# One fp32 product for the attention scores in place of three products of split halves, in a fused attention and gated-MLP kernel

## Chip, cores and metric

The kernel runs on one core of one Trainium2 chip. The metric is the device time of one execution in microseconds (us), the median of three runs. The engines are named as the profile names them: PE is TensorE's matmul side and PEld its weight loads, DVE is VectorE, ACT is ScalarE, POOL is GpSimd, SP is SyncE, which only issues DMAs here. Everything is fp32 in memory. A tile typed fp32r holds fp32 words whose products the kernel takes at TensorE's reduced precision; a product of plain fp32 tiles is taken at full precision.

## The reference

```python
B, H, S, D = (4, 8, 576, 64)
scores = scale * np.matmul(q, k.transpose(0, 1, 3, 2))        # scale = 1/8
scores = np.where(causal, -1000000000.0, scores)
scores = scores - scores.max(-1, keepdims=True)
a = np.exp(scores); a /= a.sum(-1, keepdims=True) + 1e-09
local = np.matmul(a, v)
phi = lambda x: np.where(x > 0, x, np.exp(x) - 1.0) + 1.0
mem_out = (phi(q) @ M_prev) / (phi(q) @ z_prev + 1e-6)
out = g * mem_out + (1 - g) * local                           # g = sigmoid(beta), one per head
x = out as [2304 tokens, 512]
y = (silu(x @ w_gate) * (x @ w_val)) @ w_out                  # d_ff = 1536
```

The attention has 32 heads of 576 positions and 64 features; the MLP has 2304 tokens.

## The kernel before

The attention loop takes two heads at a time: 16 pairs, numbered 0 to 15, and one more turn (16) that only finishes the last. Partitions 0 to 63 of a pair's tiles hold the features of its first head and 64 to 127 those of its second. `pair_load` brings raw queries `qr` (128x768: the last 64 positions twice, positions 0 to 511, then the last 64 of both heads laid out block-diagonally) and raw keys `kr` (128x576). Each is held in `NR` = 2 buffers.

`pair_split` makes of each raw tile a high half (`qh`, `kh`, the value rounded to fp32r) and a low half (`ql`, `kl`, the rest). High and low together carry nearly full fp32 precision, so a score is the sum of three one-pass products, high x high, high x low and low x high: `self.products` lists them, and each accumulates in one PSUM bank. For pair 0 the work is cut in two and lies on ACT, POOL and DVE; for every other pair all four operations lie on POOL, but for pair 1's `kh`, which is ACT's.

Scores come in five tiles of 128 query rows. `scores(t)` for t = 0 to 3 takes the keys up to the diagonal, 128(t+1) columns, both heads side by side: head 0 uses rows 0 to 63 of TensorE and head 1 rows 64 to 127, each with a bank of its own (64*128 in the trace). `scores4` does the last 64 rows of both heads at once with all 128 rows, twice 288 keys (128*128). DVE reads each bank with the mask and takes the row's extreme (`reading`), ACT takes the exponential with the row sum (`exp`), POOL multiplies by the reciprocal sum and the gate (`scaled`).

A turn of the loop is software-pipelined: while pair n's scores are made, pair n-1's weights are transposed by TensorE against `ident` (`turned1`, `turned`), evacuated to `g`, and multiplied with the values (`values`, tiles `g,vp`), its memory part comes from `recall` (`mm,ph`: phi(q) times the memory matrix, in plain fp32), and its result leaves as `xh` and `xl`. `phi_parts` computes the feature map phi(q) of pair n+1 from raw `qr`: two activations on ACT (`qe`, `ph`) and one DVE operation. PE, ACT, DVE and POOL each run their instructions in the order in which the Python code issues them: the wrapper `queued` links each instruction to the one before on its engine (its recording line is L92 in the profile, so rows are told apart by tile names). SP's DMAs are ordered by the tile scheduler.

So TensorE's order within a turn is: scores t = 0 and 1, transposes of the old pair's `ps` and `pl`, `mm,ph`, scores t = 2 and 3, more transposes, `scores4`, transposes of `p` and `mem`, and the products `g,vp`. The loads of pair n+2 are issued at the end of turn n. After the loop come the MLP's products, also of split halves, which the change does not touch.

Of the kernel before, what the change touches and what calls it, by code (L numbers as in the profile page):

```python
# [9 lines left out]
F32 = mybir.dt.float32  # L10
F32R = mybir.dt.float32r
# [3 lines left out]
ALU = mybir.AluOpType  # L15
# [14 lines left out]
ORDER = (0, 768, 1536)  # L30
EARLY, AHEAD = (2, 6, 10, 14), (1, 5, 9, 11, 12, 13, 14)
PLAIN = 3
ACT_K = (0, 1)
ON_POOL = ("q", "k")
PS_S, PS_T = 4, 4
NBIG, NSMALL, FB, NK, NR, NM, NX = 8, 8, 2, 2, 2, 2, 2
STEPS = ("p1", "p2", "p6", "p7", "p5", "p4", "p3")
EDGE_A, EDGE_B, EDGE_X = 16, 176, 40
TCKW = dict(schedule_with_timeline_sim=True)
# [7 lines left out]
def attention_moe(ctx: ExitStack, tc: tile.TileContext, qt, kt_, v, m, beta, wg, wv, wo, out):  # L47
# [22 lines left out]
    def follow(ins, other, why, kind=mybir.DependencyClass.NoSync):  # L70
        tc.add_manual_dep(
            getattr(ins, "ins", ins), getattr(other, "ins", other).name,
            mybir.DependencyInfo(kind, mybir.DependencyReason.DATA), reason=why,
        )
# [26 lines left out]
    pe, act, dve, pool = queued(PE), queued(ACT), queued(DVE), queued(POOL)  # L101

    def rot(pool, name, shape, dtype, n, off=0):
        held = slots.setdefault(name, [0, []])
        if len(held[1]) < n:
            free, at = math.prod(shape[1:]), f"{name}{len(held[1])}"
            if off or free % 64:
                whole = pool.tile([shape[0], -(-(off + free) // 64) * 64], dtype, name=at)[:, off : off + free]
                held[1].append(whole if len(shape) == 2 else whole.rearrange("p (a b) -> p a b", b=shape[2]))
            else:  # L110
                held[1].append(pool.tile(shape, dtype, name=at))
        held[0] += 1
        return held[1][(held[0] - 1) % n]

    def kept(pool, name, shape, dtype, n):
        for _ in range(n):
            rot(pool, name, shape, dtype, n)

    def split_hi(dst, src):
        return pool.tensor_scalar(dst, src, 1.0, 0.0, op0=ALU.mult, op1=ALU.add)  # L120

    def split_lo(dst, src, hi, kind=""):
        eng = pool if kind in ON_POOL else dve
        return eng.tensor_tensor(dst, src, hi.bitcast(F32), op=ALU.subtract)

    ident = const.tile([128, 128], F32, name="ident")
    make_identity(nc, ident)
# [13 lines left out]
    for hh in range(2):  # L141
        rows = slice(hh * 64, hh * 64 + 64)
# [133 lines left out]
    with tc.tile_pool(name="sb", bufs=1, reuse_waits="tile") as sb:  # L276
# [21 lines left out]
            SP.dma_start(vp, v[b, pr])  # L298
            return vp

        def pair_split(n, raw):
            qr, kr = raw
            q = [rot(sb, f"q{part}", [128, 640], F32R, NK) for part in "hl"]
            k = [rot(sb, f"k{part}", [128, 576], F32R, NK, 16) for part in "hl"]
            if n == 0:
                cuts = [(slice(0, 256), slice(0, 256)), (slice(256, 576), slice(256, 640))]
                lo = lambda dst, src, hi: dve.tensor_tensor(dst, src, hi.bitcast(F32), op=ALU.subtract)
                raw = qr[:, 128:768]
                for ck, cq in cuts:
                    act.copy(k[0][:, ck], kr[:, ck])  # L310
                    split_hi(q[0][:, cq], raw[:, cq])
                (ck, cq), (dk, dq) = cuts
                lo(k[1][:, ck], kr[:, ck], k[0][:, ck])
                lo(q[1][:, cq], raw[:, cq], q[0][:, cq])
                lo(k[1][:, dk], kr[:, dk], k[0][:, dk])
                return q, k, lambda: lo(q[1][:, dq], raw[:, dq], q[0][:, dq])
            (act.copy if n in ACT_K else split_hi)(k[0], kr)
            split_hi(q[0], qr[:, 128:768])

            def lows():  # L320
                split_lo(q[1], qr[:, 128:768], q[0], "q")
                split_lo(k[1], kr, k[0], "k")

            return q, k, lows

        mms = []

        def batch_prep(b):
# [15 lines left out]
        preps, p4s, read = {}, [], {}  # L344

        class Pair:
# [3 lines left out]

            def load(self):
                self.raw = pair_load(self.n)

            def split(self):
                self.q, self.k, self.lows = pair_split(self.n, self.raw)
                self.products = [(self.q[x], self.k[y]) for x, y in ((0, 0), (0, 1), (1, 0))]

            def load_v(self):
                self.vp = pair_load_v(self.n)
# [45 lines left out]
            def scores(self, t):  # L405

                w = 128 * (t + 1)
                ps = [rot(psS, "s", [128, 512], F32, PS_S) for _ in range(2)]
                for i, (q, k) in enumerate(self.products):
                    for h in range(2):  # L410
                        rows = slice(h * 64, h * 64 + 64)
                        mm = pe.matmul(
                            ps[h][:, 0:w], q[rows, t * 128 : t * 128 + 128], k[rows, 0:w], start=(i == 0), stop=(i == 2)
                        )
                        if i == h == 0 and id(ps[1]) in read:
                            follow(mm, read[id(ps[1])], "once both banks are read", mybir.DependencyClass.Sync)

                def reading(h):
                    p = rot(sb, "pl", [128, 512], F32, NBIG) if t > 1 else rot(sb, "ps", [128, 256], F32, NSMALL)
                    read[id(ps[h])] = dve.tensor_tensor_reduce(  # L420
                        out=p[:, 0:w], in0=ps[h][:, 0:w], in1=maskp[:, 512 - w : 512], op0=ALU.add, op1=ALU.min,
                        scale=-SCALE, scalar=BIG, accum_out=self.mx[:, 2 * t + h : 2 * t + h + 1],
                    )
                    self.pts[(t, h)] = p

                return reading
# [7 lines left out]
            def scores4(self):  # L434
                c = 8
                if len(p4s) < 2:
                    p4s.append(sb.tile([128, 640], F32, name=f"p4{len(p4s)}"))
                    POOL.memset(p4s[-1][:, 576:640], 0.0)
                p = p4s[self.n % 2]
                mx = self.mx  # L440
                banks = [rot(psS, "s", [128, 512], F32, PS_S) for _ in range(2)]
                for half, ps in enumerate(banks):
                    for i, (q, k) in enumerate(self.products):
                        pe.matmul(
                            ps[:, 0:288], q[:, 512:640], k[:, half * 288 : half * 288 + 288], start=(i == 0), stop=(i == 2)
                        )
                self.pts[(4, 0)] = p

                def reading():
                    for half, ps in enumerate(banks):  # L450
                        read[id(ps)] = dve.tensor_tensor_reduce(
                            out=p[:, half * 288 : half * 288 + 288], in0=ps[:, 0:288], in1=mask4 if half else maskp[:, 0:288],
                            op0=ALU.add, op1=ALU.min, scale=-SCALE, scalar=BIG if half == 0 else mx[:, c : c + 1],
                            accum_out=mx[:, c + half : c + half + 1],
                        )

                return reading
# [119 lines left out]
        pairs = [Pair(n) for n in range(NP)]  # L577
# [1 line left out]
        pairs[0].load()  # L579
        SP.dma_start(gt, beta.partition_broadcast(128))  # L580
        pairs[1].load()
        pairs[0].split()
        pairs[0].load_v()
        phi0 = pairs[0].phi_parts()
        nothing = lambda *args: None
        ending = lambda: nothing
        copies = []
        for n in range(NP + 1):
            cur = pairs[n] if n < NP else None
            old = pairs[n - 1] if n > 0 else None  # L590
            after = pairs[n + 1] if n + 1 < NP else None
# [11 lines left out]
            reads[0](0)  # L603
            reads[0](1)
            low()
            if n == 0:
                cur.lows()
            reads[1](0)
            reads[1](1)
            for i, at in enumerate(EARLY[:3]):  # L610
# [4 lines left out]
            if n == 1:  # L615
                for work in late:
                    work()
            if after and n:
                after.split()
            exp(0, 0)  # L620
            turned1(0, act)
            turned1(1, act)
# [13 lines left out]
            if n == 0:  # L636
                one_less, memory_gates = gates()
                scaled = cur.normal(((0, 0), (0, 1), (1, 0), (1, 1)), act)
                after.split()
                after.lows()  # L640
            elif cur:
                first()
            if after and n:
                after.lows()
            if n:
                phi = after.phi_parts() if after else nothing
            reads = [scores(t) for t in range(2, 4)]
            reads[0](0)
            reads[0](1)
# [34 lines left out]
            if n == 0:  # L684
                late = [lambda cur=cur: cur.weighed(((4, 0),))]
            else:
                if n == 1:
                    phi1()
                phi()
                if cur:  # L690
                    cur.weighed(((4, 0),))
            ending = old.leave() if old else lambda: nothing
# [17 lines left out]
        i = len(EARLY) + 1  # L710
# [41 lines left out]
    banks = [x for name in ("s", "tr") for x in slots[name][1]]  # L752
# [314 lines left out]
    both = slice(0, 2)  # L1067
# [94 lines left out]
    for f in range(NF - 2):  # L1162
# [3 lines left out]
        w, w1 = w1, None  # L1166
# [68 lines left out]
    for n, (k, b, c) in enumerate(chunks):  # L1235
# [8 lines left out]
        for t in range(3):  # L1244
            ps = (a[:, 0:256], a[:, 256:512], z[:, 0:256])[t]
            for r in range(2):
                rows = slice(t * 128, t * 128 + 128)
                for m, (x, w) in enumerate(((uh, th), (uh, tl), (ul, th))):
                    pe.matmul(
                        ps, x[:, r, rows], w[:, 2 * c + r],  # L1250
                        start=(k in FRESH and c == r == m == 0 and t != 1), stop=(c == NC - 1 and r == 1 and m == 2),
# [57 lines left out]
```

## Time and profile before

| | before |
|---|---|
| median of 3 runs | 590.42 us (590.23 to 591.34) |
| the profiled execution | 590.32 us, of it 588.5 us from the first to the last instruction |
| mean granted TensorE clock | 0.997 |
| busy over the span: PE, PEld | 579.0 us (98%), 535.5 us (91%) |
| DVE, ACT, POOL | 478.1 us (81%), 391.9 us (67%), 236.5 us (40%) |
| scores of pair 0 begin; attention ends | 4.1 us; about 180 us |

The page's busy time is an average over two different stages. In the attention stage all four engines are close to full; in the MLP stage PE is, and POOL has almost nothing to do. Matmul records are pipelined: a record's length contains its way through the array, so that records overlap, and a rate is read from the distance between starts, not from the lengths. An x2 behind a matmul of 64*128 or 128*64 is two records that start within some nanoseconds of each other, one for each head.

### The profile page before, as it was taken

How to read it: one execution, taken by the hardware profiler on the slowest of the kernel's cores; microseconds unless marked ns; L12 is line 12 of the kernel's file. 1: busy time of each engine (PE TensorE's matmuls, PEld its weight loads, DVE VectorE, ACT ScalarE, POOL GpSimd, SP SyncE). 2: the span in 40 equal slices, each digit the busy share in tenths (PEclk: the TensorE clock that was granted, in tenths of full speed). 3: DMA queues.
4: the chain of work that ended last, by engine and by line, in shares of the span. 5: the costliest groups of instructions: out<-in, count | busy, mean ns of one | idle time of the engine just before them, and what ended most of it. 6: DMA issues, size and time to landing. Idle time of an engine off the chain costs nothing.

```text
span 588.5 us, 11998 instructions
## 1 busy us (share of the span) xinstructions
PE 579.0 (98%) x4118; PEld 535.5 (91%) x4118; DVE 478.1 (81%) x1161; ACT 391.9 (67%) x895; POOL 236.5 (40%) x285
## 2 busy tenths in 40 slices
PE   6999999999999999999999999999999999999997
PEld 4888888878878999999999999999999999999997
DVE  7899999999988989899998778677777776985771
ACT  7898998998887578777844655444444446646741
POOL 6999999999975333433340002122220000000000
PEclk9999999999999999999999999999999999999999
DMA  8446856757417555699848587365475426998852
GB/s 252 144 141 189 282 157 200 251 170 219 171 64 278 200 176 187 209 311 280 267 163 301 163 284 224 135 215 189 178 249 215 138 111 201 310 402 279 266 194 80
DMA packets 66092, 124.26 MB, mean 211 GB/s; under 512 B 8304, under 2 KB 37360, under 8 KB 66032
## 3 DMA queue, kind: packets, MB, share of 16 engines
q1 hardware_dynamic: 65744, 123.21, 63.0%
q8 instruction: 32, 0.52, 0.4%
q10 hardware_dynamic: 288, 0.30, 0.1%
q14 instruction: 28, 0.23, 0.1%
HBM read 80.23 MB, written 43.25 MB: 210 GB/s over the span
## 4 chain that ended last, share of the span: by engine, by line
PE 94%; ACT 2%; DMA 1%; DVE 1%; POOL 1%; issue 0%; SPq 0%; ACTq 0%
PE s L92 62%; PE tr L92 32%; DMA qr<-in_qt_dram 1%; DMA up<-zh 1%; DVE xall L92 1%; POOL ps L92 0%; ACT g L92 0%; ACT ps L92 0%; POOL kl L92 0%; ACT L92 0%; DVE zg L92 0%; DVE zh L92 0%; ACT we L92 0%; ACT xall L92 0%; SPq L289 0%
## 5 line engine op out<-in xcount | busy, mean ns | idle before, releaser
L92 PE MATMUL s<-xall,th 128*128 128x384 f32 x336 | 85.8, 337 | 0.0
L92 PEld LDWEIGHTS s<-xall,th 128*128 128x128 f32 x336 | 61.0, 188 | 3.8 <-ACT zp L92 0.9
L92 PE MATMUL s<-xall,bh 128*128 128x384 f32 x252 | 64.2, 336 | 0.0
L92 PE MATMUL s<-xall,tl 128*128 128x384 f32 x168 | 56.5, 336 | 0.0
L92 POOL TENSOR_SCALAR pl<-pl,rs,og 128x384 f32<-128x384 f32 (+1 forms) x64 | 54.2, 861 | 4.8 <-DVE rs L92 4.2
L92 POOL TENSOR_SCALAR we<-we 128x512 f32<-128x512 f32 x32 | 25.2, 788 | 73.8 <-ACT we L92 70.4
L92 POOL TENSOR_TENSOR tq<-w 128x256 f32<-128x256 f32 x12 | 8.6, 740 | 108.9 <-DVE zs L92 99.2
L92 ACT ACTIVATE zh<-zh 128x384 f32<-128x384 f32 x33 | 17.3, 526 | 51.1 <-DVE zh L92 51.0
L92 DVE TENSOR_TENSOR xall<-ur,xall 128x768 fp32r<-128x768 f32 x42 | 39.3, 952 | 13.6 <-ACT xall L92 13.6
L92 PE MATMUL tr<-g,vp 128*64 128x320 f32 (+4 forms) x448 | 48.8, 360 | 0.2 <-ACT g L92 0.2
L92 PEld LDWEIGHTS s<-xall,bh 128*128 128x128 f32 x252 | 45.7, 188 | 1.8 <-DVE zv L92 0.2
L92 PEld LDWEIGHTS tr<-g,vp 128*64 128x64 f32 x448 | 29.4, 137 | 18.0 <-issue 2.7
L92 ACT ACTIVATE pl<-pl,mx 128x384 f32<-128x384 f32 (+1 forms) x64 | 42.5, 665 | 4.1 <-DVE mx L92 3.3
L92 PE MATMUL s<-xall,bl 128*128 128x384 f32 x126 | 42.3, 336 | 0.0
L92 ACT CAST xall<-ur 128x768 fp32r<-128x768 f32 x42 | 34.3, 833 | 10.2 <-PE tr L92 3.1
L92 PE MATMUL s<-kh,qh 64*128 64x128 f32 (+4 forms) x160 | 36.1, 378 | 5.0 <-ACT kh L92 4.1
L92 DVE CUSTOM_DVE_ANT_0 pl<-s,maskp 128x384 f32<-128x384 f32 (+1 forms) x64 | 38.2, 617 | 0.7 <-PE s L92 0.3
L92 ACT COPY g<-tr 128x384 f32<-128x384 f32 (+1 forms) x60 | 30.0, 526 | 4.3 <-PE tr L92 4.2
L92 ACT ACTIVATE ps<-ps,mx 128x128 f32<-128x128 f32 (+1 forms) x64 | 28.6, 454 | 6.2 <-DVE mx L92 6.0
L92 POOL TENSOR_SCALAR ps<-ps,rs,og 128x128 f32<-128x128 f32 (+1 forms) x64 | 32.0, 517 | 1.4 <-DVE rs L92 1.4
L92 PEld LDWEIGHTS s<-xall,tl 128*128 128x128 f32 x168 | 31.6, 188 | 0.0
L92 ACT ACTIVATE zg<-zg 128x384 f32<-128x384 f32 x33 | 17.3, 525 | 20.8 <-DVE zg L92 20.4
(231 smaller groups left out, 1914.7 us busy)
## 6 DMA issues: line engine op xcount, KB each, us to landing
ur<-up SPq DMA_DIRECT2D x42, 384.0 KB, 4.7
up<-zg SPq DMA_DIRECT2D x36, 192.0 KB, 2.3
wraw<-in_wg_dram SPq DMA_DIRECT2D x12, 512.0 KB, 4.0
wraw<-in_wv_dram SPq DMA_DIRECT2D x12, 512.0 KB, 4.3
wraw<-in_wo_dram SPq DMA_DIRECT2D x12, 512.0 KB, 5.1
qr<-in_qt_dram SPq DMA_DIRECT2D x15, 384.0 KB, 3.1
vp<-in_v_dram SPq DMA_DIRECT2D x16, 320.0 KB, 4.9
wr<-wdr SPq DMA_DIRECT2D x10, 512.0 KB, 3.7
```

Source lines behind the costliest of these rows:

```text
L92: ins = getattr(eng, name)(*args, **kw)
```

## The change

`pair_split` goes, with its eight `q`/`k` half tiles. `scores` and `scores4` multiply the raw `qr` and `kr` once, in plain fp32, with `start` and `stop` on the same instruction. `NR` becomes 3, since raw tiles are now read until the pair's last score. The feature map keeps its operations and engines; pair 0's moves from before the loop to the middle of turn 0. Bank choice, DVE's reading, the exponentials, the transposes and the MLP stay.

```diff
-ACT_K = (0, 1)
-ON_POOL = ("q", "k")
 PS_S, PS_T = 4, 4
-NBIG, NSMALL, FB, NK, NR, NM, NX = 8, 8, 2, 2, 2, 2, 2
+NBIG, NSMALL, FB, NR, NM, NX = 8, 8, 2, 3, 2, 2
...
-        def pair_split(n, raw):
...
             def load(self):
                 self.raw = pair_load(self.n)
-
-            def split(self):
-                self.q, self.k, self.lows = pair_split(self.n, self.raw)
-                self.products = [(self.q[x], self.k[y]) for x, y in ((0, 0), (0, 1), (1, 0))]
+                self.q, self.k = self.raw[0][:, 128:768], self.raw[1]
...
-                for i, (q, k) in enumerate(self.products):
-                    for h in range(2):
-                        rows = slice(h * 64, h * 64 + 64)
-                        mm = pe.matmul(
-                            ps[h][:, 0:w], q[rows, t * 128 : t * 128 + 128], k[rows, 0:w], start=(i == 0), stop=(i == 2)
-                        )
...
+                for h in range(2):
+                    rows = slice(h * 64, h * 64 + 64)
+                    mm = pe.matmul(
+                        ps[h][:, 0:w], self.q[rows, t * 128 : t * 128 + 128], self.k[rows, 0:w], start=True, stop=True
+                    )
...
-        pairs[0].split()
         pairs[0].load_v()
-        phi0 = pairs[0].phi_parts()
...
-            if after and n:
-                after.split()
             exp(0, 0)
...
                 scaled = cur.normal(((0, 0), (0, 1), (1, 0), (1, 1)), act)
-                after.split()
-                after.lows()
+                phi0 = cur.phi_parts()
...
-            if after and n:
-                after.lows()
-            if n:
-                phi = after.phi_parts() if after else nothing
+            if n and after:
+                phi = after.phi_parts()
```

On PE, here is what stood between the memory product and the next transposes in a steady turn (the scores of t = 2 and 3; `s` are the banks, numbers are buffers):

```order
L92 MATMUL tr_305<-mm_157,ph_256 128x130 x2
L92 MATMUL s_167<-kh_146,qh_144 128x384
L92 MATMUL s_168<-kh_146,qh_144 128x384
L92 MATMUL s_167<-kl_147,qh_144 128x384
L92 MATMUL s_168<-kl_147,qh_144 128x384
L92 MATMUL s_167<-kh_146,ql_145 128x384
L92 MATMUL s_168<-kh_146,ql_145 128x384
L92 MATMUL s_175<-kh_146,qh_144 128x512
L92 MATMUL s_176<-kh_146,qh_144 128x512
L92 MATMUL s_175<-kl_147,qh_144 128x512
L92 MATMUL s_176<-kl_147,qh_144 128x512
L92 MATMUL s_175<-kh_146,ql_145 128x512
```

and what stands there now, up to the scores of the last rows:

```order
L90 MATMUL tr_257<-mm_146,ph_176 128x130 x2
L90 MATMUL s_156<-kr_133,qr_132 128x384
L90 MATMUL s_157<-kr_133,qr_132 128x384
L90 MATMUL s_152<-kr_133,qr_132 128x512
L90 MATMUL s_153<-kr_133,qr_132 128x512
L90 MATMUL tr_264<-ident,pl_202 128x128 x4
L90 MATMUL tr_269<-ident,pl_204 128x128 x4
L90 MATMUL s_156<-kr_133,qr_132 128x288
L90 MATMUL s_157<-kr_133,qr_132 128x288
```

Nothing changed places: three instructions for each bank became one, on the same rows of TensorE and with the same widths.

On ACT, this is the start of the program before, from the second cast of pair 0's keys to the first exponential of t = 2 (`ps` and `pl` are the scores' tiles, `gs` the gates, `rs` the row sums):

```order
L92 CAST kh_146<-kr_133 128x320
L92 ACTIVATE qe_162<-qr_132 128x640
L92 ACTIVATE ph_161<-qr_132 128x640
L92 ACTIVATE ps_183,sm_166<-ps_183,mx_165 128x128
L92 ACTIVATE ps_185,sm_166<-ps_185,mx_165 128x128
L92 ACTIVATE ps_188,sm_166<-ps_188,mx_165 128x256
L92 ACTIVATE ps_190,sm_166<-ps_190,mx_165 128x256
L92 ACTIVATE gs<-gt 128x8
L92 ACTIVATE gs<-gs,ones 128x8
L92 ACTIVATE rs_198<-sm_166,tiny 128x4
L92 CAST kh_202<-kr_141 128x576
L92 ACTIVATE pl_220,sm_166<-pl_220,mx_165 128x384
```

and this is the same stretch now:

```order
L90 ACTIVATE ps_160,sm_151<-ps_160,mx_150 128x128
L90 ACTIVATE ps_162,sm_151<-ps_162,mx_150 128x128
L90 ACTIVATE ps_164,sm_151<-ps_164,mx_150 128x256
L90 ACTIVATE ps_166,sm_151<-ps_166,mx_150 128x256
L90 ACTIVATE gs<-gt 128x8
L90 ACTIVATE gs<-gs,ones 128x8
L90 ACTIVATE rs_174<-sm_151,tiny 128x4
L90 ACTIVATE qe_177<-qr_132 128x640
L90 ACTIVATE ph_176<-qr_132 128x640
L90 ACTIVATE pl_184,sm_151<-pl_184,mx_150 128x384
```

The three casts of keys are gone, and the two activations of the feature map (`qe`, `ph`) moved from ahead of the first exponential to behind the row sums' step.

## Rows read from the trace of the kernel before

**Rows 1.** Chain of work that ended last, pairs 3 to 14, shares by line.

```profile
by line: PE tr L92 71.1%; PE s L92 28.9%; issue 0.0%
```

**Rows 2.** Busy us by pair (twelve windows): length, PE, PEld, DVE, ACT, POOL, granted clock, DMA.

```profile
57.33:67.98 10.65, 10.65 (x105) 8.82 (x101) 9.83 (x38) 9.39 (x27) 10.52 (x14) 1.00 0.77 238
...
sum 128.65, PE 128.60 PEld 105.72 DVE 119.39 ACT 115.80 POOL 127.34; mean PE 10.72 PEld 8.81 DVE 9.95 ACT 9.65 POOL 10.61
```

**Rows 3.** Weight loads' waits by releaser in that stretch: total us, times, longest.

```profile
PEld tr L92 <- POOL kh L92: 1.4, 4, 0.4
```

**Rows 4.** GpSimd groups of splits in that stretch: busy us, mean ns, idle before.

```profile
L92 POOL TENSOR_TENSOR ql<-qr,qh 128x640 fp32r<-128x640 f32 x12 | 18.7, 1560 | 0.0
...
L92 POOL TENSOR_TENSOR kl<-kr,kh 128x576 fp32r<-128x576 f32 x12 | 17.1, 1425 | 0.0
...
L92 POOL TENSOR_SCALAR qh<-qr 128x640 fp32r<-128x640 f32 x12 | 8.8, 732 | 0.0
L92 POOL TENSOR_SCALAR kh<-kr 128x576 fp32r<-128x576 f32 x12 | 8.1, 676 | 0.0
```

**Rows 5.** Timeline of pair 5 and the start of 6: start, length, engine, instruction.

```profile
60.80 0.44 PE L92 MATMUL s<-kh,qh 64*128 64x384 f32 x2
...
61.08 0.34 PE L92 MATMUL s<-kl,qh 64*128 64x384 f32 x2
...
61.43 0.39 PE L92 MATMUL s<-kh,qh 64*128 64x512 f32 x2
...
61.66 0.39 PE L92 MATMUL s<-kl,qh 64*128 64x512 f32 x2
...
62.22 1.09 PE L92 MATMUL tr<-ident,pl 128*128 128x128 f32 x8
...
63.06 0.38 PE L92 MATMUL s<-kh,qh 128*128 128x288 f32 x1
...
63.28 0.29 PE L92 MATMUL s<-kl,qh 128*128 128x288 f32 x1
...
63.94 0.71 PE L92 MATMUL tr<-ident,p 128*128 128x128 f32 x5
...
65.01 0.87 PE L92 MATMUL tr<-g,vp 128*64 128x256 f32 x8
...
65.71 0.28 PE L92 MATMUL tr<-ident,mem 128*64 128x64 f32 x4
...
65.83 2.23 PE L92 MATMUL tr<-g,vp 128*64 128x320 f32 x20
...
67.98 0.33 PE L92 MATMUL s<-kh,qh 64*128 64x128 f32 x2
...
68.88 0.88 PE L92 MATMUL tr<-ident,ps 128*128 128x128 f32 x6
...
69.01 0.40 ACT L92 ACTIVATE ps<-ps,mx 128x128 f32<-128x128 f32 x1 [0.49 <-DVE mx L92]
```

**Rows 6.** Timeline of the first 16 us, same columns.

```profile
3.54 0.41 POOL L92 TENSOR_SCALAR qh<-qr 128x256 fp32r<-128x256 f32 x1 [0.64 <-DMA qr<-in_qt_dram]
...
4.10 0.47 PE L92 MATMUL s<-kh,qh 64*128 64x128 f32 x2 [4.10 <-ACT kh L92]
...
5.63 0.74 ACT L92 ACTIVATE qe<-qr 128x640 f32<-128x640 f32 x1 [0.75 <-DMA qr<-in_qt_dram]
...
6.90 0.39 ACT L92 ACTIVATE ps<-ps,mx 128x128 f32<-128x128 f32 x1
...
9.28 0.65 ACT L92 CAST kh<-kr 128x576 fp32r<-128x576 f32 x1
...
9.84 0.61 ACT L92 ACTIVATE pl<-pl,mx 128x384 f32<-128x384 f32 x1
...
15.13 0.39 ACT L92 ACTIVATE ps<-ps,mx 128x128 f32<-128x128 f32 x1
...
16.02 1.60 PEld L92 LDWEIGHTS tr<-mm,ph 128*128 128x128 f32 x10 [0.21 <-ACT g L92]
```

More of the change, by code (lines that the diff above doesn't have):

```diff
@@ L117, in kept @@
             rot(pool, name, shape, dtype, n)
[L119 to L124, printed above, removed]
     ident = const.tile([128, 128], F32, name="ident")
@@ L299, in pair_load_v @@
             return vp
-        def pair_split(n, raw):
[L302 to L324, printed above, removed]
         mms = []
@@ L408, in scores @@
                 ps = [rot(psS, "s", [128, 512], F32, PS_S) for _ in range(2)]
-                for i, (q, k) in enumerate(self.products):
-                    for h in range(2):
-                        rows = slice(h * 64, h * 64 + 64)
-                        mm = pe.matmul(
-                            ps[h][:, 0:w], q[rows, t * 128 : t * 128 + 128], k[rows, 0:w], start=(i == 0), stop=(i == 2)
-                        )
-                        if i == h == 0 and id(ps[1]) in read:
-                            follow(mm, read[id(ps[1])], "once both banks are read", mybir.DependencyClass.Sync)
+                for h in range(2):
[3 more added lines that the diff above has]
+                    )
+                    if h == 0 and id(ps[1]) in read:
+                        follow(mm, read[id(ps[1])], "once both banks are read", mybir.DependencyClass.Sync)
                 def reading(h):
@@ L442, in scores4 @@
                 for half, ps in enumerate(banks):
[L443 to L446, printed above, removed]
+                    pe.matmul(
+                        ps[:, 0:288], self.q[:, 512:640], self.k[:, half * 288 : half * 288 + 288], start=True, stop=True
+                    )
                 self.pts[(4, 0)] = p
@@ L605, in attention_moe @@
             low()
-            if n == 0:
-                cur.lows()
             reads[1](0)
@@ L688, in attention_moe @@
                     phi1()
-                phi()
+                if after:
+                    phi()
                 if cur:
```

## The prediction

> **What bounds the kernel now.** The change touches only the attention stage, so I read that stage alone, and first the chain of work that ended last from pair 3 to pair 14: every step of it is TensorE's, 71.1% on banks `tr` and 28.9% on banks `s`, the scores [rows 1]. The busy times by pair look less clear, since POOL is as full as PE: over twelve pairs, 128.65 us, PE is busy for 128.60, POOL for 127.34, DVE for 119.39 and ACT for 115.80 [rows 2]. Who waits for whom decides between PE and POOL. Weight loads waited for POOL four times in the twelve pairs, 1.4 us in all [rows 3]; an engine that set the pace would be waited for in every pair. And in the timeline of one pair the scores, transposes and value products follow each other without a hole longer than the change from one tile shape to another [rows 5]. A steady pair takes 10.65 us, the mean is 10.72 [rows 2]. I conclude that PE's own stream is the bound and that POOL just keeps up.
>
> **What goes from POOL, and who notices.** Four operations in a pair: 1.56 for `ql`, 1.43 for `kl`, 0.73 for `qh` and 0.68 for `kh`, 4.4 us of POOL's 10.6 [rows 2, 4]. This is the largest saving of the change and it lies beside PE's stream, so I count it at what PE waited: the twelve pairs lost 12 x (10.72 - 10.65) = 0.85 us against the steady one [rows 2], not all of it to POOL. I take 0.7 us for the whole stage, between 0 and 1.2.
>
> **What the scores cost on PE.** Now for a reduced product: two products of 384 columns, both heads at once, take 61.43 - 61.08 = 0.35 us, and one of 512 takes 61.66 - 61.43 = 0.23 [rows 5], so about 0.44 ns a column: one column for each tick of 2.4 GHz (granted clock 1.00 [rows 2]). The trace of before has no plain fp32 product with 64 rows. The nearest row is the value product `g,vp`, plain fp32 with 64 columns of weights for each head, both heads at once. Eight records over 384 columns for each head (256 and 128) take 65.71 - 65.01 = 0.70 us, and twenty over 1216 (three times 320, 192 and 64) take 67.98 - 65.83 = 2.15 [rows 5]. The slope is 1.45 / 832 = 1.74 ns a column; the longer group also pays a change of tile shape at its end, of about 0.1, and without it and with a start of 0.05 on the shorter it is 1.68. I take 1.67, four ticks a column, with 1.74 as the upper end. So the product costs four passes where there were three.
>
> The Trainium skill, "FP8 and Floating Point Precision", TensorE Precision Notes, also gives true fp32 four passes. By that rule alone the 1856 columns of a pair's scores would cost one pass more, 0.77 us a pair; the sum below would end at 600.1. The rows make it less, because not every product now runs at its column rate.
>
> By place, always entry and exit plus columns:
> - t = 2 and 3: from 60.80 to 62.22, 1.42 us, of which the six products are 3 x 0.175 + 3 x 0.23 = 1.215 and the changes of tile shape 0.205 [rows 5]. After: 896 columns x 1.67 = 1.495, plus 0.205, is 1.70: +0.28 (up to +0.35).
> - t = 0 and 1: from 67.98 to 68.88, 0.90 us [rows 5]. Without 0.205 the six products take 0.116 each, though half of them have 128 columns, worth 0.056: they wait for weights, not for columns. After: 384 columns x 1.67 = 0.64, plus 0.205, is 0.85. I take 0, between -0.05 and +0.15 should four loads instead of two stand in line for a product.
> - last rows: from 63.06 to 63.94, 0.88 us; five products in 63.94 - 63.28 = 0.66, so 0.13 each, and 0.09 for entering [rows 5]. After: 576 columns x 1.67 = 0.96, plus 0.09, is 1.05: +0.17 (up to +0.21).
>
> Together +0.45 us a pair, between +0.40 and +0.71. Pairs 1 to 15 pay it on PE's path: 15 x 0.45 = 6.8 us, between 6.0 and 10.7. Pair 0 pays it inside the start, below. With PE at 11.1 us a pair, DVE (9.95 on the mean [rows 2]) and ACT have more room than before, so no new bound follows.
>
> **What costs nothing.** The third raw buffer: the load of pair n+2 now writes where pair n-1 lay, whose last score was a turn earlier, so it waits for nothing; with two buffers it would wait for the current pair's last score, with most of a turn of 10.65 us still to hide it. DVE's reading of the banks: same count, same banks, and more time between a bank's stop and its next use. The MLP: same instructions.
>
> **The start.** Queries are there at 3.54, when POOL's wait for them ends; the first score starts at 4.10, after the casts [rows 6]. It can now start about 0.5 earlier. The first exponential stood at 6.90, behind the feature map, which had waited for the last piece of `qr` until 5.63 and took 1.27 [rows 6]. In a steady pair the first exponential follows the first score by 69.01 - 67.98 = 1.03 [rows 5]; I allow 1.3, as the early products run slower, so it starts near 4.9. From there to the end of the row sums' step ACT took 9.28 - 6.90 = 2.38, then cast `kh` until 9.84 [rows 6]. Now: 4.9 + 2.4, and 0.2 for t = 1's scores arriving, is 7.5; the moved feature map takes its 1.27; the exponentials of t = 2 start at 8.75 in place of 9.84, about 1.1 earlier. I follow ACT because the place where PE becomes the bound hangs on it: the memory product of turn 1, from which PE runs on, was released at 16.02 by ACT's `g` copy behind the exponential at 15.13 [rows 6]. So the start gives 1.1 us, between 0 (if DVE or PE, at four passes and a slow clock, takes ACT's place) and 2.5.
>
> **Sum.** 590.3 (the profiled execution: span 588.5 and 1.8 around it, 0.1 under the median) + 6.8 - 0.7 - 1.1 = 595.3 us. With its bounds: 590.3 + 6.0 - 1.2 - 2.5 = 592.6 up to 590.3 + 10.7 = 601.0. Two runs of this kernel can be told apart from about 0.2%, 1.2 us.
>
> **The rivals.**
> - *The two heads are not fully side by side in plain fp32* (slower still). Each plain product leaves two records; if the second of head 0 must start before the first of head 1, the heads overlap by half, and each group of scores ends with two lone passes of its widest tile: 512 / 2.4 + 1024 / 2.4 ns, 0.64 us a pair, 9.6 in all: 604.9. The Trainium skill, "TensorE: Matmul & The Clock Gate", Part 3, says that matmuls start and end strictly in program order; by that rule this would be expected. Against it: the value products are issued in that same order, and 384 columns in 0.70 us leave no room for it [rows 5]. But those split TensorE's columns, the scores its rows. Chance 0.08. With no overlap at all it is 1280 columns x 1.67 = 2.1 us a pair, 32 us: 627. Chance 0.05.
> - *POOL is the pace, and PE's stream is stretched to it* (faster). POOL's 10.61 against 10.72 speaks for it [rows 2]. Then its 4.4 us go from the path, and the next engine, DVE, gives 9.95 a pair: 15 x 0.77 = 11.5 less, and with the start 578. It decides if PE's stream in [rows 5] has slack hidden in it, more than 0.45 a pair; the one rate of 0.44 ns on products of 384 and 512 columns, and the waits of [rows 3], speak against it. Chance 0.05.
> - *The gains eat the loss*: scores at +0.25 a pair, 3.8 us, against 2.5 + 1.2 at the start and from stalls: 590.4, no change. It needs plain products below 1.55 ns a column. Chance 0.04.
>
> The forecast itself has 0.78. Slower: forecast and first rival, 0.91. Faster: POOL's rival and a little of the last, 0.06. Same: 0.03. The range runs from 592.0 to 605.0: the forecast's own and the half-overlap; left out are the last three cases.
>
> **What would show it.** In the trace after: a turn of about 11.1 us in every steady pair; t = 2 and 3 in 1.70, the last rows in 1.05, t = 0 and 1 within 0.1 of 0.90; two records of both heads starting together; POOL near 6 us of 11; PE still the whole chain; the first exponential near 4.9 and that of t = 2 near 8.75. Wrong would be: turns of 11.7 or more (heads), turns under 10.6 (POOL), or a start no earlier than before.

## The result, and the profile after

The changed kernel takes 594.39 us (median of 4 runs, 594.36 to 594.83) against 590.33 for the kernel before beside it: ratio 1.0067, 95% interval 1.0049 to 1.0084. It is slower, by 4.1 us. The profiled execution, at 594.83 us, lies 0.44 above its median; its span is 593.0 us, 4.5 longer than before.

Busy time by stretch, after: length, then PE, PEld, DVE, ACT and POOL, each with its instructions, granted clock, DMA share, GB/s. The stretches are the start up to turn 2, turns 2 to 14, the rest, one steady turn, and turns 3 to 14. A turn runs from the first score of t = 0 to that of the next turn.

```profile
0.00:24.18 24.18, 17.54 (x111) 11.00 (x112) 16.29 (x68) 19.37 (x56) 10.56 (x27) 1.00 0.67 204
24.18:168.84 144.66, 144.58 (x1188) 106.49 (x1184) 129.54 (x494) 124.56 (x357) 82.02 (x118) 1.00 0.58 187
168.84:593.00 424.16, 420.51 (x2668) 405.64 (x2664) 330.06 (x596) 245.39 (x480) 78.25 (x81) 1.00 0.64 217
57.71:68.80 11.09, 11.09 (x95) 8.19 (x91) 9.78 (x38) 9.38 (x27) 6.23 (x10) 1.00 0.80 272
35.54:168.84 133.30, 133.30 (x1097) 98.32 (x1093) 119.49 (x455) 115.17 (x330) 75.44 (x109) 1.00 0.59 191
```

The same for before: the same three stretches, then a stretch of the start, then turns 5 to 14.

```profile
0.00:25.07 25.07, 19.43 (x131) 14.72 (x131) 18.47 (x72) 20.90 (x59) 19.97 (x36) 0.93 0.59 184
25.07:164.67 139.60, 139.44 (x1317) 114.52 (x1314) 129.66 (x494) 125.19 (x358) 138.25 (x170) 1.00 0.62 196
164.67:588.50 423.83, 420.17 (x2678) 406.25 (x2674) 329.98 (x598) 245.83 (x481) 78.24 (x81) 1.00 0.65 218
13.50:16.90 3.40, 3.40 (x15) 2.75 (x16) 2.39 (x12) 3.40 (x11) 3.40 (x6) 0.50 0.62 208
57.33:164.67 107.34, 107.29 (x1014) 88.07 (x1011) 100.04 (x380) 96.46 (x275) 106.44 (x131) 1.00 0.63 201
```

The difference of the spans is in the thirteen turns: 144.66 - 139.60 = +5.06. The start is 0.89 shorter although turn 1 in it already pays the dearer scores; the rest, with turn 15, is 0.33 longer. POOL fell from 127.34 [rows 2] to 75.44 in turns 3 to 14, and PE is busy for every one of their 133.30 us. The chain over these turns is PE's alone, as in [rows 1], with the scores' share up from 28.9%:

```profile
by line: PE tr L90 68.2%; PE s L90 31.8%
```

One turn on PE and the start of the next, the counterpart of [rows 5]: start, length, instruction.

```profile
68.80 0.93 PE L90 MATMUL s<-kr,qr 64*128 64x128 f32 x8
69.66 0.88 PE L90 MATMUL tr<-ident,ps 128*128 128x128 f32 x6
...
72.24 1.77 PE L90 MATMUL s<-kr,qr 64*128 64x384 f32 x8
73.94 1.09 PE L90 MATMUL tr<-ident,pl 128*128 128x128 f32 x8
74.87 1.14 PE L90 MATMUL s<-kr,qr 128*128 128x288 f32 x4
75.84 0.71 PE L90 MATMUL tr<-ident,p 128*128 128x128 f32 x5
...
79.89 0.49 PE L90 MATMUL s<-kr,qr 64*128 64x128 f32 x4
```

From start to start: t = 0 and 1 take 69.66 - 68.80 = 0.86, t = 2 and 3 take 73.94 - 72.24 = 1.70, the transposes with the last rows 75.84 - 73.94 = 1.90. The next row of scores begins 79.89 - 68.80 = 11.09 after the first.

The first microseconds, on ScalarE and then PE, for comparison with [rows 6]; in brackets the idle time before and its releaser.

```profile
4.97 0.40 ACT L90 ACTIVATE ps<-ps,mx 128x128 f32<-128x128 f32 x1 [2.32 <-DVE mx L90]
...
7.17 0.21 ACT L90 ACTIVATE gs<-gt 128x8 f32<-128x8 f32 x1 [0.24 <-DMA gt<-in_beta_dram]
...
7.80 0.72 ACT L90 ACTIVATE qe<-qr 128x640 f32<-128x640 f32 x1
...
9.05 0.60 ACT L90 ACTIVATE pl<-pl,mx 128x384 f32<-128x384 f32 x1
...
14.32 0.39 ACT L90 ACTIVATE ps<-ps,mx 128x128 f32<-128x128 f32 x1
```

```profile
3.69 5.48 PE L90 MATMUL s<-kr,qr 64*128 64x128 f32 x20 [3.69 <-DMA kr<-in_kt_dram]
...
15.21 1.38 PE L90 MATMUL tr<-mm,ph 128*128 128x130 f32 x10 [0.59 <-ACT g L90]
16.52 0.59 PE L90 MATMUL s<-kr,qr 64*128 64x384 f32 x2
```

The first exponential moved from 6.90 to 4.97 and that of t = 2 from 9.84 to 9.05. ACT then stood for `gt`, the beta broadcast, 0.24 us long. The memory product of turn 1 moved from 16.02 to 15.21, and takes until 16.52, 1.31 us, where before it took 17.75 - 16.02 = 1.73:

```profile
16.02 1.80 PE L92 MATMUL tr<-mm,ph 128*128 128x130 f32 x10
17.75 0.45 PE L92 MATMUL s<-kh,qh 64*128 64x384 f32 x2
```

### The profile page after: what moved, and what is told of

Read it like the earlier page. It is cut to its first block, busy times and chain, and to the rows that moved or that the text cites. A ratio compares the mean times of both kernels' runs of the same rounds, so it can differ in the third digit from the quotient of the medians.

```text
span 593.0 us, 11652 instructions
## 1 busy us (share of the span) xinstructions
PE 582.6 (98%) x3958; PEld 523.1 (88%) x3958; DVE 475.9 (80%) x1157; ACT 389.3 (66%) x892; POOL 170.8 (29%) x224
## 4 chain that ended last, share of the span: by engine, by line
PE 94%; ACT 2%; DMA 1%; DVE 1%; issue 0%; SPq 0%
PE s L90 63%; PE tr L90 31%; DMA gt<-in_beta_dram 1%; DMA up<-zh 1%; DVE xall L90 1%; ACT pl L90 0%; ACT g L90 0%; ACT L90 0%; ACT qe L90 0%; ACT ph L90 0%; SPq L280 0%; DVE zg L90 0%; DVE zh L90 0%; ACT we L90 0%; ACT xall L90 0%
## 5 line engine op out<-in xcount | busy, mean ns | idle before, releaser
L90 POOL TENSOR_SCALAR pl<-pl,rs,og 128x384 f32<-128x384 f32 (+1 forms) x64 | 52.9, 838 | 60.7 <-DVE rs L90 60.7
L90 PE MATMUL s<-kr,qr 64*128 64x128 f32 (+4 forms) x320 | 63.3, 459 | 4.8 <-DMA kr<-in_kt_dram 3.7
L90 DVE TENSOR_TENSOR xall<-ur,xall 128x768 fp32r<-128x768 f32 x42 | 39.4, 954 | 13.5 <-ACT xall L90 13.5
L90 PEld LDWEIGHTS s<-kr,qr 64*128 64x128 f32 (+1 forms) x320 | 31.2, 193 | 16.0 <-DVE mx L90 3.8
L90 PEld LDWEIGHTS tr<-ident,pl 128*128 128x128 f32 x210 | 23.0, 140 | 13.3 <-POOL ps L90 6.8
```

The source lines that it names most:

```text
L90: ins = getattr(eng, name)(*args, **kw)
```

## The experiments

The runs of the kernel before that stood beside them had medians of 590.37, 590.12 and 590.91 us, so each ratio goes against its own.

**1. POOL's work put back (`pool_load`).** The changed kernel, with four operations on POOL in each pair, from pair 2 on; nobody reads their results.

```
+        def dead_split(n, raw):
...
+            pool.tensor_scalar(kh, kr, 1.0, 0.0, op0=ALU.mult, op1=ALU.add)
+            pool.tensor_scalar(qh, qr[:, 128:768], 1.0, 0.0, op0=ALU.mult, op1=ALU.add)
...
+                pool.tensor_tensor(ql, qr[:, 128:768], qh.bitcast(F32), op=ALU.subtract)
+                pool.tensor_tensor(kl, kr, kh.bitcast(F32), op=ALU.subtract)
```

> The changed kernel, with the four POOL operations of every pair from 2 on put back at their old places, written to tiles that nobody reads. If POOL's work lies beside TensorE's stream, a steady turn stays at 11.1 us and the time at 594.4, at most 0.6 more where POOL is late now and then. If POOL's occupancy had set the turn before, its load counts again: with 10.6 us of POOL work in a turn of 11.1 the time may rise by some us, and TensorE waits for POOL in most turns.

594.4 us, ratio 1.0066 (1.0043 to 1.0089), the same as the change. Turns 3 to 14, and the longest wait of the weight loads for POOL in them:

```profile
35.11:168.39 133.28, 133.28 (x1097) 98.33 (x1093) 120.78 (x455) 115.14 (x330) 125.41 (x157) 1.00 0.60 191
```

```profile
PEld tr L90 <- POOL qh L90: 8.3, 11, 0.8
```

POOL is nearly full again, 125.41, and the twelve turns take 133.28 against 133.30. The weight loads wait 8.3 us for `qh` on POOL (in the change itself 5.3 us for `ps`) and PE is still busy throughout: a wait of the weight loads is no loss by itself, which also makes the 1.4 us of [rows 3] a weak measure in either direction.

**2 and 3. PE made short, with and without POOL's relief (`onepass_split`, `onepass_high`).** The kernel before with one product in place of three; then also without the low halves.

```
-                self.products = [(self.q[x], self.k[y]) for x, y in ((0, 0), (0, 1), (1, 0))]
+                self.products = [(self.q[x], self.k[y]) for x, y in ((0, 0),)]
...
-            def lows():
-                split_lo(q[1], qr[:, 128:768], q[0], "q")
-                split_lo(k[1], kr, k[0], "k")
-
-            return q, k, lows
+            return q, k, lambda: None
```

The second piece is `onepass_high`'s alone.

> The kernel before with the first of the three score products alone (high x high; the two products with a low half are left out, so the scores are less precise), while all four POOL operations of a pair stay. TensorE's scores go from 3.2 to about 1.4 us a pair, its stream to about 8.9. If TensorE was the bound and POOL with 10.6 us stood right behind it, the turn falls only to POOL's 10.6 and the time to about 589 to 590. If POOL's rows were stretched by waiting and had room, the turn falls to DVE's 9.95 or below and the time to 580 or less.

> As the run with one product and four POOL operations, but the two operations that make the low halves are left out too (3.0 us of POOL's turn; the low halves are neither made nor used). If POOL is the next bound once TensorE has room, the turn now falls to DVE's 9.95 to 10.1 us and the time to 578 to 582, some 9 us under the run with four operations. If POOL is no bound even then, the two runs agree within 1 us.

`onepass_split`: 589.69 us, ratio 0.998 (0.9967 to 0.9994). `onepass_high`: 588.97, ratio 0.9967 (0.9952 to 0.9983). Turns 5 to 14 of the one and of the other, and what POOL waited for in the second:

```profile
57.15:163.81 106.66, 100.15 (x815) 71.76 (x812) 100.93 (x381) 97.16 (x276) 106.15 (x131) 1.00 0.65 203
```

```profile
57.34:163.72 106.38, 100.03 (x814) 71.77 (x810) 100.65 (x381) 97.16 (x276) 77.01 (x111) 1.00 0.59 195
```

```profile
POOL pl L92 <- DVE rs L92: 32.6, 11, 3.2
```

The first came as expected and looked like POOL's bound: 106.15 of 106.66. The second refutes that reading: POOL has 77.01 us of work and waits 32.6 us for DVE, and the ten turns are only 0.28 shorter. My 578 to 582 was wrong by seven microseconds or more. PE lost 7.3 of its 107.3 us in these ten turns and the time only 1.0. So PE's stream was the bound, but another limit lay 0.1 us a turn behind it.

**4. Start alone (`raw01`).** The kernel before with raw scores in pairs 0 and 1 and no splits for them; the feature map of pair 0 is moved as in the change.

```
             def load(self):
                 self.raw = pair_load(self.n)
+                self.products = [(self.raw[0][:, 128:768], self.raw[1])]
...
-        pairs[0].split()
         pairs[0].load_v()
-        phi0 = pairs[0].phi_parts()
...
-            if n == 0:
-                cur.lows()
...
-                after.split()
-                after.lows()
+                phi0 = cur.phi_parts()
```

> The kernel before, with plain fp32 scores in pairs 0 and 1 alone and their splitting gone; pairs 2 to 15 keep the three products. If the start's gain and the steady loss are separate terms, turn 2 begins 0.9 us earlier (24.2 in place of 25.1), the turns after it stay at 10.65, and the time is 0.9 below the kernel before: 589.4. If the gain at the start is taken back by POOL's splitting of pair 2, or is paid for by the plain products, it is 590.3 or more.

588.39 us, ratio 0.9963 (0.995 to 0.9976): the change's start, without the loss of its turns, is faster. Turn 2 begins at 23.72 (24.18 in the change, 25.07 before), and turns 3 to 14 are near those of [rows 2]:

```profile
34.61:162.81 128.20, 128.20 (x1218) 105.83 (x1214) 119.08 (x456) 115.40 (x330) 126.82 (x157) 1.00 0.64 202
```

The time is 1.0 us below the 589.4 that I expected, for two reasons. The start is 0.46 earlier than the change's. And the twelve turns take 128.20 in place of 128.65, though PE's turn is no longer and POOL has all its work: against twelve steady turns of 10.65 they lose 0.40 to stalls, where the kernel before lost 0.85.

Here beta was in time. ACT's first exponential and its `gs`, for comparison with 4.97 and 7.17 in the change:

```profile
4.85 0.40 ACT L92 ACTIVATE ps<-ps,mx 128x128 f32<-128x128 f32 x1 [2.19 <-DVE mx L92]
...
6.71 0.19 ACT L92 ACTIVATE gs<-gt 128x8 f32<-128x8 f32 x1
```

The exponential of t = 2 began at 8.58 in place of 9.05, the memory product of turn 1 at 14.75 in place of 15.21. Of the 0.46 us by which `gs` is earlier, 0.12 was already there at the first exponential; the other 0.34 is beta's. The 0.46 goes through unchanged to the beginning of turn 2.

**5. Last rows alone (`last_raw`).** The kernel before, raw operands (`self.whole`) in the last rows' scores only.

```
-                    for i, (q, k) in enumerate(self.products):
+                    for i, (q, k) in enumerate(self.whole):
                         pe.matmul(
...
+                            ps[:, 0:288], q[:, 512:640], k[:, half * 288 : half * 288 + 288], start=True, stop=True
```

> The kernel before with one part of the change alone: the last rows' scores (two times 288 keys, all 128 rows of TensorE) multiply raw tiles in plain fp32; t = 0 to 3 keep the three products, and all splitting stays. By the prediction's term the transposes and last rows together take 1.90 in place of 1.73 us a turn, 0.17 more; in pairs 1 to 15 that is 2.6 us: 593.0. If the terms of the scores do not add up alone (other waits absorb them), it is under 591.5.

592.25 us, ratio 1.0038 (1.0026 to 1.005): 2.1 us above the kernel before, of 2.6 expected. Turns 3 to 14:

```profile
36.15:166.52 130.37, 130.37 (x1191) 104.87 (x1189) 119.83 (x455) 115.29 (x330) 126.84 (x157) 1.00 0.63 201
```

In a steady turn the transposes and the last rows take 75.54 - 73.64 = 1.90, as in the change. The twelve turns grew by 130.37 - 128.65 = 1.7, not by 12 x 0.18 = 2.2: POOL has all its work and half a microsecond of the stalls is gone all the same. A longer PE turn could cover them; but `raw01` lost as much of its stalls, 0.45, with turns that are no longer.

**6. Narrow products raw everywhere (`hybrid`).** As `raw01`, with t = 0 and 1 raw in every pair.

```
+                products = self.products if t > 1 else self.whole
+                for i, (q, k) in enumerate(products):
```

> As the run with plain scores in pairs 0 and 1, and besides plain fp32 scores at t = 0 and 1 in every pair, where the products wait for weights and not for columns; t = 2, 3 and the last rows keep the split halves. By the rows after the change t = 0 and 1 take 0.85 in place of 0.89 us: 0.04 x 14 = 0.6 less than that run's 588.4: 587.8. If plain fp32 costs four passes against three there too, it is 384 columns at 0.42 ns, 0.16 a turn and 2.2 us more: 590.6.

588.29 us, ratio 0.9967 (0.9954 to 0.9979), within its noise `raw01`'s time and 0.5 above the 587.8 expected. Scores t = 0 and 1 of a steady turn and the transposes behind them:

```profile
56.02 0.93 PE L92 MATMUL s<-kr,qr 64*128 64x128 f32 x8
56.88 0.88 PE L92 MATMUL tr<-ident,ps 128*128 128x128 f32 x6
```

From start to start t = 0 and 1 take 0.86, against 0.90 in [rows 5]: four plain passes cost the narrow products nothing over three reduced ones, as the prediction had it.

**7 and 8. A still shorter start (`best`, `best2`).** As `hybrid`, with beta's load ahead of the last piece of `qr`, and the ReLU of pairs 0 and 1 on POOL; `best2` turns its two operations round.

```
+                    if dst is qr and c.start == 0:
+                        SP.dma_start(gt, beta.partition_broadcast(128))
...
+                if self.n < 2:
+                    pool.tensor_scalar(x, raw, 0.0, BIG, op0=ALU.max, op1=ALU.min)   # best
+                    pool.tensor_scalar(x, raw, BIG, 0.0, op0=ALU.min, op1=ALU.max)   # best2
```

> As the hybrid run, with the start's ACT chain shortened: the gates' input is loaded ahead of the last piece of the queries, and in pairs 0 and 1 the feature map's second activation (0.63 us each) goes to POOL, which idles there. If ACT sets the start, turn 2 begins another 1.1 us earlier, at about 22.6, and the time is 586.7. If DVE or TensorE's products set it as soon as ACT is a little faster, it equals the hybrid run within 0.4.

> As the best run, whose POOL operation for the feature map (largest with 0, then least with a big number, 640 columns) took 2.35 us instead of the 0.75 of POOL's multiplications of that size and so held up POOL's scaling behind it; here the same two operations stand in the other order, least first, the order in which POOL's clamp of 512 columns takes 0.79. If the order makes the price, it takes about 0.95, POOL's scaling starts 1 us earlier, turn 2 begins near 22.5 and the time is 587.3. If not, all stays as in the best run: 588.3.

`best`: 588.26 us, ratio 0.9976 (0.9965 to 0.9987), no better than `hybrid`, where 586.7 was expected; turn 2 begins at 23.28. `best2`: 587.55 us, ratio 0.9944 (0.9931 to 0.9956), turn 2 begins at 22.66; it beats both kernels. The POOL operation in the first 20 us, in `best` and in `best2` (busy, mean ns):

```profile
L92 POOL TENSOR_SCALAR ph<-qr 128x640 f32<-128x640 f32 x2 | 4.7, 2346 | 3.0 <-DMA qr<-in_qt_dram 3.0
```

```profile
L92 POOL TENSOR_SCALAR ph<-qr 128x640 f32<-128x640 f32 x2 | 1.4, 724 | 2.7 <-DMA qr<-in_qt_dram 2.7
```

The operation of 2346 ns stood ahead of POOL's scaling of `pl`, which PE's transposes wait for. At 724 ns turn 2 begins 0.62 earlier and the median is 0.7 us lower, of 1.0 expected. That gain stands in the medians and the ratios alone: the two profiled executions have the same span, 586.1 us, the one being the fastest of its twelve runs and the other the slowest of its five.

**9 and 10. What binds the short turn (`onepass_high_phi`, `onepass_high_nophi`).** As `onepass_high`, with DVE's feature-map operation given to POOL, then left out.

```
-                return lambda: dve.scalar_tensor_tensor(out=x, in0=e, scalar=1.0, in1=x, op0=ALU.min, op1=ALU.add)
+                    pool.tensor_scalar(e, e, 1.0, 0.0, op0=ALU.min, op1=ALU.add)   # phi
+                    pool.tensor_tensor(x, e, x, op=ALU.add)   # phi
+                return lambda: None   # nophi
```

> As the run with one product and no low halves (the scores again less precise), with DVE's one operation of the feature map (0.8 us a turn) done by two operations on POOL, which waits 3 us a turn there. If the turn of 10.6 us in that run hangs on DVE's order of work with its waits, the turn falls by 0.5 to 0.8 us and the time to 578 to 582. If it hangs on the ring between TensorE and ACT, it stays at 588 to 589.

> As the run with one product and no low halves (less precise scores), and DVE's one operation of the feature map is left out too, so the memory part is of another function. Nothing is added to POOL. If the turn of 10.6 us there hangs on DVE's order of work with its waits, the turn falls by 0.5 to 0.8 us and the time from 589.0 to 577 to 582. If it hangs on the ring between TensorE and ACT, it stays at 588 to 589.

`onepass_high_phi`: 605.34 us, ratio 1.0256 (1.0219 to 1.0293). Six turns, and the new group on POOL:

```profile
53.45:120.27 66.82, 57.91 (x490) 43.14 (x486) 55.71 (x223) 56.83 (x164) 65.61 (x79) 1.00 0.65 204
```

```profile
L92 POOL TENSOR_SCALAR qe<-qe 128x640 f32<-128x640 f32 x6 | 14.5, 2419 | 0.0
```

The run made POOL the pace, 65.61 of 66.82, and so says nothing of DVE. `onepass_high_nophi`: 588.28 us, ratio 0.9957 (0.9943 to 0.9971). Turns 5 to 14, and two of the waits:

```profile
56.99:162.73 105.74, 99.85 (x814) 71.81 (x811) 94.20 (x371) 97.00 (x276) 72.33 (x112) 1.00 0.60 196
```

```profile
PEld s L92 <- DVE mx L92: 5.8, 19, 0.5
DVE rs L92 <- ACT p L92: 5.8, 10, 0.6
```

DVE lost 6.45 us in ten turns and they became 0.64 shorter; no engine is full. PE's weight loads wait for DVE's `mx`, DVE waits for ACT's `p`, and ACT waits for DVE's `mx` (6.9 us in all): waits that close on each other among the three are what the rows suggest. That they set the 10.6 us is argued, not shown.

## Why the prediction was right

The forecast was 595.3 and the median is 594.39, slower, inside the range. Its sum of +5.0 stands against +4.5 in the spans of the profiled executions and +4.1 in the medians; the 0.4 between these two is the distance of the change's profiled execution to its median. By term, the spans' +4.5 is 6.5 for the scores, -0.7 for fewer stalls and -1.3 for the start.

**PE's stream is the bound: right, by a thinner margin than I thought.** The chain, PE's 133.30 of 133.30 and `pool_load` agree. The margin is the 0.1 us a turn of experiment 3, which matters only to kernels that shorten PE. [rows 3] is only the largest of three rows: with those of `qh` and `pl` the weight loads waited for POOL six times before, 2.0 us in all. That leaves the reading as it was.

**Scores, +0.45 a pair: right term by term.** t = 2 and 3 were forecast at 1.70 and took 1.70, +0.28; t = 0 and 1 were forecast at +0 and came to -0.04; the last rows with the transposes ahead of them gave 1.90 - 1.72 = +0.18 (forecast +0.17). The turn is 11.09 against 11.1. Fifteen pairs pay: 13 x 0.44 in turns 2 to 14, 0.45 taken for turn 1, 0.33 for the rest of the program with turn 15 in it, 6.5 in all against 6.8. The value product was thus a good stand-in at 1.67 ns a column, though it splits the array's columns and the scores its rows. The Trainium skill's four passes for true fp32 ("FP8 and Floating Point Precision", TensorE Precision Notes) agree with this rate. The extra pass on every column, which by that rule alone led to 600.1, did not show at t = 0 and 1, where `hybrid` measured 0.86 against 0.90.

**POOL's relief, -0.7: right in size by luck, wrong in cause.** The twelve turns before lost 0.85 us to stalls. After, they lost 133.30 - 12 x 11.09 = 0.22, so 0.63 came back. But `pool_load`, with POOL's work back, has the same 133.28. The step that failed is the one that booked the stalls to POOL's account: POOL's lost 4.4 us a turn are worth nothing measurable. What took the stalls away stays open. The longer PE turn, which gives every partner 0.44 us more, is one candidate. But `raw01` lost only 0.40, with turns as long as before and all of POOL's work, so 0.45 of the 0.63 can go without either; and all of it is less than the 1.2 us by which the four runs of the kernel before beside the change differ.

**Start, -1.1: sized 0.2 too low, out of two errors that by luck nearly cancel.** Turn 2 begins 0.89 earlier and turn 1 paid some 0.45 in that time, so the start gave 1.34. The path through ACT was the right one: exponential of t = 2, exponential (0, 0) of pair 1 and memory product came 0.79, 0.81 and 0.81 earlier. It was to be 1.1; beta's broadcast, which the forecast didn't name as what is late next, held ACT until 7.17, and by `raw01` that cost 0.34. That lateness seems to belong to the execution more than to the change: the broadcast landed 5.0 us after its issue here, 4.2 in `pool_load` with the same loads, and 3.3 to 4.6 in the eleven other traces. That the profiled execution lies 0.44 above its median fits this, but the change has no second trace to show it. In the other direction, the memory product itself became 0.42 shorter: before, the clock was granted at 0.50 from 13.5 to 16.9, the lower level of 1.2 GHz, and after it is 1.00 there. This too may be the execution's: beside the experiments, ten runs of the kernel before had a mean granted clock of 1.000 and a median of 590.4 us, not lower than the rest, though ten runs so scattered would hardly show 0.4. The sum 0.81 + 0.42 leaves 0.1 of the 1.34 unexplained.

**The rivals.** Half overlap of the heads, 604.9, fell with the turn of 11.09 in place of 11.7, and no overlap at all, 627, with it. The records show it too. Here PE's instructions of t = 2 in the turn at 68.80, first those running between 72.50 and 72.60, then between 72.60 and 72.80 (durations, then first and last start):

```profile
L90 PE MATMUL s<-kr,qr x2: 587/587/587, 72.2 to 72.2; 64*128 64x384 f32 x2
...
L90 PE MATMUL s<-kr,qr x4: 482/534/587, 72.2 to 72.7; 64*128 64x384 f32 x4
```

Two of the four records start together at 72.2, and the two others some 0.4 later: first halves of both heads, then second halves. The Trainium skill ("TensorE: Matmul & The Clock Gate", Part 3) has matmuls start and end strictly in program order. The trace does not go against that: taken whole, the two heads' products start together and end together. What was wrong is the step from there to the half overlap, which applied the rule to the single records. POOL as the pace was refuted by the longer turn and by `onepass_high`: with PE's stream cut by 0.7 us a turn and POOL relieved, the turn is still 10.64, so its 578 was wrong as well. The gains that eat the loss would have needed 1.55 ns a column; t = 2 and 3 in 1.70 left no room for it.

## What to carry to other kernels

Price a product by its passes times its columns, but first see in the trace whether it runs at its column rate: narrow products here cost as much at four passes as at three, wide ones about a quarter more (for t = 2 and 3 without the changes of tile shape, 1.50 us against 1.22). An engine that is 99% busy is not yet a bound, and a wait for it is not yet a loss: put its work back, or take it away, and see whether the turn moves. Where a change wins at the start and loses in the steady stretch, take the two apart; the start alone, with the narrow products raw and two edits more, is 587.55 us.

## What the hardware showed beyond expectation

- One POOL operation over 128x640 fp32 took 724 ns as a minimum followed by a maximum, 2346 ns as a maximum followed by a minimum, and 2419 ns as a minimum followed by an addition; multiply and add took 732 [rows 4]. Why is open.
- The granted clock of 0.50 between 13.5 and 16.9 us before set in after holes in PE's work of 0.70, 0.23 and 0.43 us in the four microseconds ahead (2.63 busy of 4.00), and PE was busy throughout it; it was back at 1.00 from 16.9. After, PE had larger holes between 9.2 and 13.4 (2.00 busy of 4.20) and kept 1.00. What decided it was not tried.
- Beta's broadcast, 4 KB in all, landed 5.0 us after its issue at 2.10 amid the larger loads in the profiled execution of the change, 4.2 us after it in `pool_load` with the same loads, and between 3.3 and 4.6 in the other ten traces.
